# The running maximum's last two steps of an attention kernel, with the ninth chunk's scores in PSUM as an operand of both

## The chip, the core and the metric

The kernel runs on one core of a Trainium2 chip. A core has TensorE (PE in the profile; PEld is its loading of weights), VectorE (DVE), ScalarE (ACT), GpSimd (POOL) and SyncE (SP, which here issues all DMAs), a memory SBUF that all engines use and a small memory PSUM into which PE writes its results. The metric is the time of one execution on the device in microseconds, the median of the runs; lower is better.

## What is computed

The reference is an attention with pooled queries, followed by a soft mixture of experts. Eight batches of eight heads, 1152 keys, 64 elements; the queries are averaged in pairs, so 576 of them are left.

```python
q_pool = q.reshape(B, H, S // factor, factor, D).mean(axis=3)
scores = scale * np.matmul(q_pool, k.transpose(0, 1, 3, 2))
scores = scores - np.max(scores, axis=-1, keepdims=True)
attn = np.exp(scores)
attn = attn / (np.sum(attn, axis=-1, keepdims=True) + 1e-09)
return np.matmul(attn, v).astype(np.float32)
```

The result, 4608 rows of 512, is the x of the mixture: `logits = x @ phi`, a softmax over the rows that gathers x into 32 slots, two matrix products with a ReLU between for each of eight experts, and a softmax over the slots that spreads the result over the rows. All data are 32-bit floats. The maximum of the scores over the keys is the part that the change touches.

## The kernel before

**Units.** Two heads are worked on together, which makes 32 pairs; the 576 queries of a pair are cut into three thirds of 192. A pair's third is a unit: there are 96, and each has scores of 1152 keys by 2 heads by 192 queries. The keys lie on the 128 partitions, in nine chunks of 128, so that one chunk is a block of 128 x 2 x 192 = 128 x 384 numbers.

**A unit's steps**, by the short names of the graph and the methods of class `Unit`:

- `S` (`scores`): PE makes the scores of a tile of chunks in PSUM. The tiles are chunks (0, 1), (2, 3), (4, 5), (6, 7) and (8). There are two PSUM buffers for them, `sc0` and `sc1`, of two banks each, taken in turn. So a tile waits until all that work on the tile two before it are done.
- `C` (`copy`): ACT copies the tile to SBUF, into `s`.
- `X` (`maxi`, L523 to L531): DVE keeps a running maximum `M`, a tile in SBUF with two parts of 384, one for the even and one for the odd chunks. The second tile is compared with the copy of the first, the third and fourth from PSUM with `M`. The ninth chunk stands alone and is compared with the first part, `M[:, 0]`.
- `Xf` (`fold`, L533): DVE folds the two parts of `M` into `M[:, 0]`. In the order of before it stands between the fourth tile and the ninth chunk.
- `mt`, `mc`, `mb` (`max_cols`, `max_red`, `max_rows`): PE transposes the 384 maxima of each partition in three matmuls (m<-ident,M in the profile), DVE reduces them, and PE spreads the result over the partitions.
- `sub`, `exp`: DVE subtracts the maximum from three chunks at a time, ACT takes the exponential.
- `add`, `sums`: GpSimd adds seven of the chunks up (cs in the profile), and PE sums over the partitions with a matrix of ones.
- `av`, `ue`: PE multiplies with the values into `U`, ACT copies the result out.
- `tc`, `eps`, `rcp`, `tr`, `nx`: the sums are turned (DVE, 32 x 32 blocks), inverted (DVE), turned back, and GpSimd multiplies them into the result `xT`.

Three score buffers `s` in SBUF let three units be under way at once.

**The mixture's first half** (class `Moe`) runs between the units, one piece for each batch of twelve units. The expert matrices are loaded into SBUF in pieces of 512 KB, 23 of the 64 during the units and the others where the units' memory comes free. What follows behind the last unit is the mixture's second half.

**The order.** No engine's order is written by hand. `graph` lists every step with its engine, a cost in a model, the steps that it depends on, and a priority: the table `K["t"]` gives a due time for each kind of step, counted from the unit's own time (9.0 us a unit). `plan` goes through the graph as a list scheduler: on each engine, of the steps that can start within `K["wait"]` of the earliest, it takes the one with the least due time; `K["stay"]` is a bonus for a PE step that keeps PE in the mode (row groups, column groups, all of it) it is in. The result is one order of all steps, and the program is written in it; each engine works through its own part strictly in that order. The waits between engines follow from what each step reads and writes.

The profile gives nearly all instructions the line of a helper (L344, the call in `InOrder`), so groups are told apart by the names of their tiles: `M<-M` is `Xf`, `M<-sc,M` with 128x384 is the ninth chunk's `X`, `M<-sc,M` and `M<-sc,s` with 128x768 are the others.

Of the kernel before, what the change touches and what calls it, by code (L numbers as in the profile page):

```python
# [12 lines left out]
ALU = mybir.AluOpType  # L13
# [9 lines left out]
K = dict(  # L23
    unit=9.0,
    bufs=3,
    stay=97.457,
    wait=dict(PE=0.13, ACT=0.445, DVE=0.179, Pool=4.882),
    adds=(7, 7, 2),
    more=3,
    tiles=((0, 1), (2, 3), (4, 5), (6, 7), (8,)),  # L30
    groups=((0, 1, 2), (3, 4, 5), (6, 7, 8)),
    t=dict(
        S=(1044.713, -27.378, 661.778, 130.467, 574.088),
        C=(225.408, -176.587, 488.066, 26.318, 184.372),
        X=(-718.744, -301.904, -170.628, 686.571, 208.197),
        Xf=(730.727,),
        mt=(148.202,),
        mc=(-195.597,),
        mb=(131.38,),
        sub=(-1080.957, -16.471, 937.631),  # L40
        exp=(-1246.656, 343.957, 478.305),
        add=(-198.042, -184.679, 499.318, 714.631, 189.507, 204.651, 492.919, -541.643, -599.421),
        av=(778.115, -59.256, -118.326, -753.912, 731.892, 755.181, 926.264, 54.633, -257.777),
        sums=(248.993, -468.15, 546.677, -343.84, -281.108, -244.636, -433.554, -1124.137, 780.762, 473.892),
        ue=(756.065,),
        tc=(-949.47,),
        eps=(-191.284,),
        rcp=(26.863,),
        tr=(550.849,),
        ad2=(-53.911, -555.751, -604.838, -526.867, -758.418, 550.551, -1200.835, -328.898, -440.675),  # L50
        nx=(106.946,),
        ldk=(-619.286,),
        ldq=(598.38,),
        ldv=(-572.603,),
        qs=(673.048,),
        lg=(-347.354, 583.603, 769.132, 771.621),
        to=(568.435, 368.579, 194.047, -715.38),
        cb=(-19.617, 862.666),
        rm=(693.434, 659.42),
        nm=(-571.082,),  # L60
        ex=(723.911,),
        ns=(-235.664,),
        ce=(449.167,),
        cz=(641.165,),
        cm=(218.808,),
        on=(-345.56, 611.94, -1045.413, -114.604, -959.343, -369.874, 674.366, 739.505, 216.76, -1205.971, -784.9,
            231.495),
        we=(175.597, 148.186),
        ga=(550.866, 285.942, 446.335),
        end_lg=(297.494, 404.708, 205.171, -617.161),  # L70
        end_to=(-1060.395, 611.733, 617.206, 387.095),
        end_cb=(452.212, 686.767),
        end_rm=(-41.937, 690.132),
        end_nm=(-764.111,),
        end_ex=(794.722,),
        end_ns=(1693.028,),
        end_ce=(-656.049,),
        end_cz=(283.723,),
        end_cm=(-111.35,),
        end_on=(-245.398, -314.311, 700.307, -568.747, 642.619, -769.575, 431.084, 234.287),  # L80
        end_we=(196.041, -1145.853),
        end_ga=(619.182, -375.889, -765.507),
        fin_lg=(193.516, 208.183),
        fin_to=(-933.237, -176.561),
        fin_cb=(677.952, 123.947),
        fin_rm=(47.158,),
        fin_nm=(-321.662,),
        fin_ex=(537.275,),
        fin_ns=(474.34,),
        fin_ce=(684.257,),  # L90
        fin_cz=(538.018,),
        fin_cm=(778.587,),
        fin_on=(655.715, -822.063, -169.447, 107.564),
        fin_we=(557.048, -643.386),
        fin_ga=(827.62, -315.564, 319.142),
        fin_gs=(-237.215,),
    ),
)
LAT = 0.05
# [12 lines left out]
def dve_t(n):  # L112
    return 0.075 + 0.001042 * n, 0.16 + 0.001042 * n
# [12 lines left out]
def graph(K, B, HP, NT3, Q, NW):  # L126
# [3 lines left out]
    TI, GR = K["tiles"], K["groups"]  # L130
# [15 lines left out]
    def op(name, eng, cost, deps=(), bank=None, take=False, give=False, key=None):  # L146
        if not isinstance(cost, tuple):
            cost = (cost, cost + (0.17 if eng == "PE" else 0.1))
        mode = MODES.get(name[0], "full") if eng == "PE" else None
        ops[name] = (eng, cost, place(*name) if key is None else key, [d for d in deps if d], bank, take, give, mode)  # L150
# [5 lines left out]
    def old(ok, *name):  # L156
        return name if ok else None
# [21 lines left out]
    for u in range(NU):  # L179
        n, na = u // NT3, adds[u]  # L180
        for i, tl in enumerate(TI):
            g = len(TI) * u + i - 2
            d = [old(g >= 0, "C", g // len(TI), g % len(TI)), old(g >= 0 and g % len(TI), "X", g // len(TI), g % len(TI))]
            d += [("S", u, i - 1)] if i else [("qs", n), ("x", "ldk", n), old(u, "S", u - 1, len(TI) - 1)]
            d += [("x", "k2")] if u == 0 and tl[0] == KF else [("qs2",)] if (u, i) == (1, 0) else []
            op(("S", u, i), "PE", 0.00168 * Q * len(tl), d)
            d = [("S", u, i)]
            for c in tl:
                d += [("av", u - NB, c), freed(u - NB, c)] if u >= NB else []
            op(("C", u, i), "ACT", act_t(2 * Q * len(tl)), d)  # L190
            if i:
                before = ("X", u, i - 1) if 1 < i < len(TI) - 1 else ("C", u, 0) if i == 1 else ("Xf", u)
                op(("X", u, i), "DVE", dve_t(2 * Q * len(tl)), [("C", u, i), before] + [old(u and i == 1, "mt", u - 1)])
            if i == len(TI) - 2:
                op(("Xf", u), "DVE", dve_t(2 * Q), [("X", u, i)])
        b = ("m", u)
        op(("mt", u), "PE", 0.33, [("X", u, len(TI) - 1)], b, take=True)
        op(("mc", u), "DVE", (0.465, 0.55), [("mt", u), old(u > 1, "mb", u - 2)], b)
        op(("mb", u), "PE", 0.34, [("mc", u)], b)
        for g, cs in enumerate(GR):  # L200
            op(("sub", u, g), "DVE", dve_t(2 * Q * len(cs)), [("mb", u)], b, give=g == len(GR) - 1)
            op(("exp", u, g), "ACT", (1.065, 1.175), [("sub", u, g)])
        for c in range(NC):
            e = [("exp", u, group_of[c])]
            if 0 < c <= na:
                d = e + ([("add", u, c - 1)] if c > 1 else [("exp", u, 0), old(u > 1, "sums", u - 2, NC)])
                op(("add", u, c), "Pool", pool_t(2 * Q), d)
            op(("av", u, c), "PE", 0.00168 * Q, e + [("av", u, c - 1) if c else old(u, "ue", u - 1), old(c == 0, "x", "ldv", n)])
        op(("ue", u), "ACT", act_t(Q), [("av", u, NC - 1), old(u, "nx", u - 1)])
        c0, end = na + 1, ("add", u, na) if na else ("exp", u, 0)  # L210
        items = []
        if u == NU - 1 and K["more"]:
            items, c0, end = [(na, end)], na + 2 + K["more"], ("ad2", u, na + 1 + K["more"])
            for c in range(na + 2, c0):
                op(("ad2", u, c), "DVE", dve_t(2 * Q), [("exp", u, group_of[c]), ("ad2", u, c - 1) if c > na + 2 else ("exp", u, group_of[na + 1])])
        items = [(c, ("exp", u, group_of[c])) for c in range(c0, NC)] + items + [(NC, end)]
        for i, (c, d) in enumerate(items):
            op(("sums", u, c), "PE", 0.00168 * Q, [d, old(i, "sums", u, items[i - 1][0])], ("n", u), take=i == 0)
        op(("tc", u), "DVE", (0.295, 0.375), [("sums", u, NC), old(u, "eps", u - 1)], ("n", u), give=True)
        op(("eps", u), "ACT", (0.2, 0.31), [("tc", u), old(u > 1, "tr", u - 2)])  # L220
        op(("rcp", u), "DVE", (0.09, 0.18), [("eps", u)])
        op(("tr", u), "DVE", (0.29, 0.375), [("rcp", u), old(u > 1, "nx", u - 2)])
        b = u // (NT3 * HP) - 2
        d = [("tr", u), ("ue", u)] + [old(b >= 0, "on", b, j, 0) for j in range(6)] + [old(b >= 0, "lg", b, j, 0) for j in range(2)]
        op(("nx", u), *(("Pool", pool_t(Q)) if u < NU - 1 else ("DVE", dve_t(Q))), d)
    for i, (b, tiles, halves) in enumerate(parts(B)):
# [7 lines left out]
        before = old(0 < i < B, "we", i - 1, 0)  # L234
# [115 lines left out]
def pooled_attention_soft_moe(ctx: ExitStack, tc: tile.TileContext, q, k, v, phi, w1, w2, out):  # L350
# [149 lines left out]
    class Unit:  # L500
# [22 lines left out]
        def maxi(self, i):  # L523
            if i == 1:
                self.M = un.tile([P, 2, 2, QU], F32, name=f"M{self.u}", tag="M", bufs=1)
            n = len(TI[i])
            ps = self.ps[i][:, :, :n * QU].rearrange("p h (c q) -> p c h q", c=n)
            if n == 2:
                dve.tensor_tensor(self.M, ps, self.s[:, 0:2] if i == 1 else self.M, op=ALU.max)
            else:  # L530
                dve.tensor_tensor(self.M[:, 0], ps[:, 0], self.M[:, 0], op=ALU.max)  # L531

        def fold(self):  # L533
            dve.tensor_tensor(self.M[:, 0], self.M[:, 0], self.M[:, 1], op=ALU.max)

        def max_cols(self, bank):
            M = self.M[:, 0].rearrange("p h q -> p (h q)")
# [426 lines left out]
```

## Time and profile before

| | before |
|---|---|
| median of three runs | 986.83 us (986.08 to 987.94) |
| the profiled execution | 987.6 us |
| its span, first to last instruction | 985.8 us |
| mean granted clock of PE | 0.992 |
| busy: PE, DVE, POOL, ACT | 951.1, 902.6, 794.9, 762.3 us |
| HBM traffic over the span | 101 GB/s |

The profile is of one execution. An engine's busy time is the sum of its instructions' spans, overlaps counted once; a group's line gives operation, output<-inputs, the shape, the number of instructions, then the busy time in us and the mean of one in ns, and behind the bar the idle time of the engine before these instructions with what ended most of it. A timeline's line gives the start in us, the time taken in us, the engine, what was done, and how many instructions were merged; a bracket holds the engine's idle time before it and who ended that. PE's ends are modelled, so a busy PE may still hold pauses.

### The profile page before, as it was taken

To read this page: it belongs to the slowest core of one execution; us is meant where nothing else is said; L and a number is where in the kernel's file an instruction comes from. 1 tells how busy PE (TensorE), PEld (TensorE's weight loads), DVE (VectorE), ACT (ScalarE), POOL (GpSimd) and SP (SyncE) were. 2 spreads that over 40 slices of the span, in tenths; PEclk is the share of its full clock that TensorE was granted. 3 is DMA by queue.
4 is the path that set the end of the run, shared out by engine and by line. 5 is a ranking of instruction groups with operands and counts; after the bars stand their busy time and mean duration, and the time that the engine had idled before them with its cause. 6 is when DMAs were issued, how large, how long until landed. Compare 5 with 4: busy or idle time off the path is not lost.

```text
span 985.8 us, 23762 instructions
## 1 busy us (share of the span) xinstructions
PE 951.1 (96%) x9358; PEld 676.1 (69%) x9358; DVE 902.6 (92%) x1307; ACT 762.3 (77%) x1120; POOL 794.9 (81%) x815
## 2 busy tenths in 40 slices
PE   6999999999999999999999999999999999999995
PEld 4666777767776777677777677777776677776542
DVE  5999999999999999999999999999999999999423
ACT  4878888888878888788878788778878788877323
POOL 2899888898889898898889988899888988888200
PEclk8999999999999999999999999999999999999998
DMA  5132232232223222223122212121221221123898
GB/s 171 49 116 82 83 116 82 84 115 74 92 71 116 94 99 88 95 70 117 52 70 73 73 49 68 55 74 52 70 74 54 68 74 49 49 90 128 320 409 339
DMA packets 27681, 101.22 MB, mean 103 GB/s; under 512 B 3505, under 2 KB 4017, under 8 KB 27569
## 3 DMA queue, kind: packets, MB, share of 16 engines
q1 hardware_dynamic: 27568, 99.69, 29.4%
q8 instruction: 74, 1.21, 0.5%
q14 instruction: 39, 0.31, 0.1%
HBM read 90.24 MB, written 9.44 MB: 101 GB/s over the span
## 4 chain that ended last, share of the span: by engine, by line
PE 84%; DVE 12%; issue 1%; ACT 0%; DMA 0%; SPq 0%; DVEq 0%; ACTq 0%
PE sc L344 32%; PE U L344 27%; PE m L344 20%; DVE M L344 7%; PE b L344 5%; DVE s L344 2%; DVE zt L344 1%; DVE mc L344 1%; DVE slot L344 0%; DVE rc L344 0%; ACT s L344 0%; DMA k<-in_k_dram 0%; PE idle L344 0%; DVE c L344 0%; DVE rr L344 0%
## 5 line engine op out<-in xcount | busy, mean ns | idle before, releaser
L344 POOL TENSOR_TENSOR cs<-cs,s 128x384 f32<-128x384 f32 x571 | 586.8, 1028 | 61.7 <-ACT s L344 26.3
L344 ACT COPY s<-sc 128x768 f32<-128x768 f32 (+1 forms) x480 | 344.6, 733 | 91.8 <-PE sc L344 86.1
L344 PE MATMUL sc<-qs,k 64*128 64x192 f32 x3456 | 389.0, 349 | 20.9 <-DVE M L344 16.3
L344 DVE TENSOR_TENSOR s<-s,m 128x1152 f32<-128x1152 f32 x288 | 382.3, 1338 | 3.3 <-PE m L344 2.3
L344 ACT ACTIVATE s<-s 128x1152 f32<-128x1152 f32 x288 | 336.2, 1168 | 45.3 <-DVE s L344 45.1
L344 PEld LDWEIGHTS sc<-qs,k 64*128 64x128 f32 x3456 | 275.6, 188 | 117.0 <-issue 73.8
L344 PE MATMUL U<-s,v 128*64 128x192 f32 x3456 | 344.6, 333 | 0.9 <-ACT Us L344 0.9
L344 PEld LDWEIGHTS U<-s,v 128*64 128x64 f32 x3456 | 227.7, 136 | 73.3 <-issue 47.6
L344 DVE TENSOR_TENSOR M<-sc,M 128x768 f32<-128x768 f32 (+1 forms) x288 | 235.3, 817 | 6.3 <-ACT s L344 2.5
L344 POOL TENSOR_TENSOR cs<-s 128x384 f32<-128x384 f32 x96 | 96.8, 1008 | 33.9 <-ACT s L344 33.8
L344 DVE TENSOR_TENSOR M<-sc,s 128x768 f32<-128x768 f32 x96 | 91.0, 947 | 4.3 <-ACT s L344 4.3
L344 DVE TENSOR_TENSOR M<-M 128x384 f32<-128x384 f32 x96 | 71.2, 742 | 0.3
L344 POOL TENSOR_TENSOR xT<-rr,Us 128x192 f32<-128x192 f32 x95 | 57.1, 601 | 12.7 <-DVE rr L344 10.2
L344 POOL TENSOR_TENSOR qs<-q 128x576 f32<-128x576 f32 x31 | 54.6, 1761 | 13.3 <-DMA q<-in_q_dram 13.3
L344 DVE TENSOR_REDUCE mc<-m 128x3 f32<-128x384 f32 x96 | 53.4, 556 | 11.4 <-PE m L344 7.4
L344 PE MATMUL m<-ident,M 128*128 128x128 f32 x288 | 52.8, 293 | 0.0
L344 PE MATMUL m<-ident,mc 128*128 128x128 f32 x288 | 51.9, 289 | 0.0
L344 PE MATMUL m<-s,ones 128*64 128x192 f32 x388 | 48.7, 330 | 0.2 <-ACT s L344 0.2
L344 PE MATMUL m<-cs,ones 128*64 128x192 f32 x384 | 47.5, 326 | 0.0
L344 ACT COPY Us<-U 128x192 f32<-128x192 f32 x96 | 30.7, 320 | 21.7 <-PE U L344 20.9
L344 PEld LDWEIGHTS m<-ident,mc 128*128 128x128 f32 x288 | 29.2, 136 | 26.6 <-DVE mc L344 24.1
L344 PEld LDWEIGHTS m<-ident,M 128*128 128x128 f32 x288 | 30.1, 141 | 21.6 <-issue 21.6
(92 smaller groups left out, 499.6 us busy)
## 6 DMA issues: line engine op xcount, KB each, us to landing
w<-in_moe_w_dram SPq DMA_DIRECT2D x64, 512.0 KB, 5.4
v<-in_v_dram SPq DMA_DIRECT2D x32, 576.0 KB, 3.8
k<-in_k_dram SPq DMA_DIRECT2D x31, 576.0 KB, 3.8
q<-in_q_dram SPq DMA_DIRECT2D x31, 576.0 KB, 3.8
out_dram<-ob SPq DMA_DIRECT2D x24, 384.0 KB, 6.0
q<-in_q_dram SPq DMA_DIRECT2D x1, 384.0 KB, 6.4
k<-in_k_dram SPq DMA_DIRECT2D x1, 320.0 KB, 4.9
k<-in_k_dram SPq DMA_DIRECT2D x1, 256.0 KB, 2.9
```

The lines of the kernel that those rows point to most:

```text
L344: return self.tc.keep_in_program_order(op(*args, **kwargs))
```

## The change

In the method for the running maximum, the ninth chunk no longer goes into `M[:, 0]`: its maximum with `M[:, 0]` is written over the scores in PSUM, and the fold then takes the maximum of that and `M[:, 1]` into `M[:, 0]`. So the ninth chunk comes ahead of the fold. In the graph, the fold now depends on the ninth chunk, the transposes on the fold, and the PSUM buffer of the ninth chunk is given back by the fold. The table of due times, the bonus `stay` and the times `wait` have new values throughout, so that the order of all steps is another. Number, shape and data of all other operations are the same.

```diff
-    stay=97.457,
-    wait=dict(PE=0.13, ACT=0.445, DVE=0.179, Pool=4.882),
+    stay=344.932,
+    wait=dict(PE=0.084, ACT=0.259, DVE=0.255, Pool=0.318),
...
-        S=(1044.713, -27.378, 661.778, 130.467, 574.088),
-        C=(225.408, -176.587, 488.066, 26.318, 184.372),
-        X=(-718.744, -301.904, -170.628, 686.571, 208.197),
-        Xf=(730.727,),
+        S=(2388.548, -94.193, 2355.419, 2292.606, -219.496),
+        C=(2649.137, 2739.454, 3306.242, 2568.215, 2210.822),
+        X=(-718.744, 41.55, 2544.783, 3038.773, 3019.567),
+        Xf=(2420.829,),
...
             d = [old(g >= 0, "C", g // len(TI), g % len(TI)), old(g >= 0 and g % len(TI), "X", g // len(TI), g % len(TI))]
+            d += [old(g >= 0 and g % len(TI) == len(TI) - 1, "Xf", g // len(TI))]
...
-                before = ("X", u, i - 1) if 1 < i < len(TI) - 1 else ("C", u, 0) if i == 1 else ("Xf", u)
+                before = ("X", u, i - 1) if i > 1 else ("C", u, 0)
                 op(("X", u, i), "DVE", dve_t(2 * Q * len(tl)), [("C", u, i), before] + [old(u and i == 1, "mt", u - 1)])
-            if i == len(TI) - 2:
-                op(("Xf", u), "DVE", dve_t(2 * Q), [("X", u, i)])
+        op(("Xf", u), "DVE", dve_t(2 * Q), [("X", u, len(TI) - 1)])
         b = ("m", u)
-        op(("mt", u), "PE", 0.33, [("X", u, len(TI) - 1)], b, take=True)
+        op(("mt", u), "PE", 0.33, [("Xf", u)], b, take=True)
...
             else:
-                dve.tensor_tensor(self.M[:, 0], ps[:, 0], self.M[:, 0], op=ALU.max)
+
+                self.top = ps[:, 0]
+                dve.tensor_tensor(self.top, self.top, self.M[:, 0], op=ALU.max)
 
         def fold(self):
-            dve.tensor_tensor(self.M[:, 0], self.M[:, 0], self.M[:, 1], op=ALU.max)
+            dve.tensor_tensor(self.M[:, 0], self.top, self.M[:, 1], op=ALU.max)
```

More of the change, by code (lines that the diff above doesn't have):

```diff
@@ L32 @@
     t=dict(
-        S=(1044.713, -27.378, 661.778, 130.467, 574.088),
-        C=(225.408, -176.587, 488.066, 26.318, 184.372),
-        X=(-718.744, -301.904, -170.628, 686.571, 208.197),
-        Xf=(730.727,),
[L37 to L96, printed above, removed]
+        S=(2388.548, -94.193, 2355.419, 2292.606, -219.496),
+        C=(2649.137, 2739.454, 3306.242, 2568.215, 2210.822),
@@ new lines @@
+        X=(-718.744, 41.55, 2544.783, 3038.773, 3019.567),
+        Xf=(2420.829,),
+        mt=(108.212,),
+        mc=(2834.326,),
+        mb=(357.261,),
+        sub=(2554.368, 2777.459, 3141.454),
+        exp=(2989.515, 2742.131, 2760.717),
+        add=(-198.042, 2806.366, 2691.244, 2455.169, 2982.071, 2750.805, 2789.269, 2832.224, -599.421),
+        av=(2746.723, 2428.358, 2392.407, 122.273, 2706.594, 2907.997, 2728.152, 193.704, -87.967),
+        sums=(248.993, -468.15, 101.759, -343.84, -281.108, -244.636, -433.554, 32.153, 2812.114, 369.166),
@@ new lines @@
+        ue=(2111.732,),
+        tc=(2995.475,),
+        eps=(-193.75,),
+        rcp=(-83.517,),
+        tr=(2755.622,),
+        ad2=(-53.911, -555.751, -604.838, -526.867, 2247.684, 2996.492, 85.086, -328.898, -440.675),
+        nx=(2766.587,),
+        ldk=(324.978,),
+        ldq=(3216.414,),
+        ldv=(-24.147,),
+        qs=(2956.952,),
+        lg=(2368.498, 2686.237, 3086.901, 182.464),
+        to=(3083.591, 2792.944, 2930.818, 2510.319),
+        cb=(2719.978, 2928.296),
+        rm=(2748.01, 258.088),
@@ new lines @@
+        nm=(2832.009,),
+        ex=(-128.418,),
+        ns=(2772.413,),
+        ce=(3121.69,),
+        cz=(2769.817,),
+        cm=(3200.587,),
+        on=(3097.6, 2506.278, 3054.228, 446.422, 2486.677, 2547.485, 2860.756, -93.424, 3100.505, 2694.192,
+            3179.786, 243.542),
+        we=(2631.977, 2680.618),
+        ga=(2926.036, 2801.7, 2712.536),
+        end_lg=(3020.693, -97.35, 2441.615, 2619.398),
+        end_to=(2726.63, -63.379, 2652.638, 2157.507),
+        end_cb=(101.937, 2494.248),
@@ new lines @@
+        end_rm=(2678.247, 2864.44),
+        end_nm=(2374.775,),
+        end_ex=(2655.735,),
+        end_ns=(2969.979,),
+        end_ce=(2929.199,),
+        end_cz=(3117.05,),
+        end_cm=(2896.398,),
+        end_on=(2567.266, 2821.336, 2621.07, 2651.936, 2871.573, 3152.89, 2747.133, 2424.348),
+        end_we=(2627.177, 2721.688),
+        end_ga=(2869.597, -375.889, 2849.104),
+        fin_lg=(2808.896, 3072.292),
+        fin_to=(2543.921, 2224.667),
+        fin_cb=(3639.957, 2729.612),
@@ L97 @@
+        fin_rm=(3023.064,),
+        fin_nm=(3006.424,),
+        fin_ex=(2881.713,),
+        fin_ns=(2929.914,),
+        fin_ce=(3322.203,),
+        fin_cz=(3098.918,),
+        fin_cm=(2739.156,),
+        fin_on=(3812.858, 3235.474, 3085.749, 2848.33),
+        fin_we=(3149.484, 2802.356),
+        fin_ga=(2993.364, -315.564, 2524.846),
+        fin_gs=(3664.586,),
     ),
```

## The prediction, made before the change was run

> **What bounds the kernel now.** I read the page first, then the windows of the middle, then the groups by form, and last the timeline unit by unit. The page's head and one window of 100 us in the middle:
>
> ```profile
> span 985.8 us, 23762 instructions
> PE 951.1 (96%) x9358; PEld 676.1 (69%) x9358; DVE 902.6 (92%) x1307; ACT 762.3 (77%) x1120; POOL 794.9 (81%) x815
> ...
> 500.00:600.00 100.00, 98.52 (x978) 71.77 (x974) 97.69 (x137) 81.94 (x117) 89.07 (x91) 1.00 0.22 67
> ```
>
> The window's columns are the stretch, its length, then busy time of PE, weight loads, DVE, ACT and POOL, the granted clock (1.00, so no throttle), DMA share and GB/s. Two engines are full at once, PE with 98.52 and DVE with 97.69 of 100 us. ACT has 18 us to spare, and DMA is idle for four fifths. Neither full engine is the answer by itself: the question is which of them sets the pace of one unit, and that cannot be read from shares. So I went to the operations that the diff touches, by form:
>
> ```profile
> L344 DVE TENSOR_TENSOR s<-s,m 128x1152 f32<-128x1152 f32 x288 | 382.3, 1338 | 3.3 <-PE m L344 2.3
> ...
> L344 DVE TENSOR_TENSOR M<-sc,M 128x768 f32<-128x768 f32 x192 | 182.3, 949 | 4.3 <-ACT s L344 2.5
> ...
> L344 DVE TENSOR_TENSOR M<-M 128x384 f32<-128x384 f32 x96 | 71.2, 742 | 0.3
> ...
> L344 DVE TENSOR_TENSOR M<-sc,M 128x384 f32<-128x384 f32 x96 | 53.1, 553 | 2.0 <-PE U L344 0.3
> ```
>
> M<-M is the fold of the maximum's two parts, both in SBUF. M<-sc,M with 384 elements is the ninth chunk, one operand in PSUM. They have the same number of elements and the same operation, yet the fold costs 742 ns against 553. The view of tile M says what kind of difference that is:
>
> ```profile
> L344 DVE TENSOR_TENSOR M<-sc,M x288: 517/951/960, 9.4 to 903.5; 128x768 f32<-128x768 f32 x96, 128x384 f32<-128x384 f32 x48
> ...
> L344 DVE TENSOR_TENSOR M<-M x96: 515/552/1360, 12.1 to 902.9; 128x384 f32<-128x384 f32 x96
> ```
>
> The three numbers are least, median and most. The fold's least and median, 515 and 552 ns, are those of the PSUM form; but some folds take up to 1360, while nothing in the first row, twice as many elements included, is over 960. So the fold is not slow: it is sometimes held up, and the operations with one operand in PSUM are not. By what, the timeline shows, GpSimd beside two folds:
>
> ```profile
> 518.42 1.01 POOL L344 TENSOR_TENSOR cs<-cs,s 128x384 f32<-128x384 f32 x1
> 519.39 1.78 POOL L344 TENSOR_TENSOR qs<-q 128x576 f32<-128x576 f32 x1
> ...
> 528.06 2.26 POOL L344 TENSOR_TENSOR cs<-cs,s 128x384 f32<-128x384 f32 x2
> ```
> ```profile
> 519.38 0.52 DVE L344 TENSOR_TENSOR M<-M 128x384 f32<-128x384 f32 x1
> 519.83 0.19 DVE L344 RECIPROCAL rc<-rc 128x6 f32<-128x6 f32 x1
> 519.93 0.55 DVE L344 TENSOR_TENSOR M<-sc,M 128x384 f32<-128x384 f32 x1
> ...
> 528.14 1.33 DVE L344 TENSOR_TENSOR M<-M 128x384 f32<-128x384 f32 x1
> ...
> 537.71 0.52 DVE L344 TENSOR_TENSOR M<-M 128x384 f32<-128x384 f32 x1
> ```
>
> The fold at 519.38 begins as a GpSimd addition ends (518.42 + 1.01 = 519.43) and takes 0.52. The one at 528.14 begins 0.08 after an addition began, and takes 1.33: the addition's time and its own. The two additions behind it take 2.26 instead of twice 1.01, so the wait goes both ways.
>
> Whether this time is on the path is settled by the pace. These are the transposes of the finished maximum, one group for each unit, and the busy time of one unit with a short fold and the next with a long one:
>
> ```profile
> 512.72 0.55 PE L344 MATMUL m<-ident,M 128*128 128x128 f32 x3
> 521.49 0.55 PE L344 MATMUL m<-ident,M 128*128 128x128 f32 x3
> 531.06 0.55 PE L344 MATMUL m<-ident,M 128*128 128x128 f32 x3
> 539.82 0.55 PE L344 MATMUL m<-ident,M 128*128 128x128 f32 x3
> ```
> ```profile
> 512.72:521.49 8.77, 8.77 (x89) 6.34 (x87) 8.63 (x13) 7.17 (x10) 7.10 (x8) 1.00 0.00 0
> 521.49:531.06 9.57, 8.97 (x88) 6.33 (x87) 9.49 (x13) 7.45 (x11) 8.93 (x11) 1.00 0.34 91
> ```
>
> The intervals are 8.77, 9.57 and 8.76 us; the folds in them took 0.52, 1.33 and 0.52. The unit is longer by 0.80 where its fold is longer by 0.81. A held-up fold is paid in full. In the long unit PE is busy for 8.97 of 9.57, with a wait of 0.60; in the short one for 8.77 of 8.77. So DVE sets the pace where the fold is held up, and PE is the floor, at about 8.77, where it is not.
>
> **The change part by part.** The profiled execution took 987.6 us, with a span of 985.8; it lies 0.8 above the median of the three timed runs, 986.83.
>
> *The fold.* It goes from two SBUF operands to one in PSUM and one in SBUF. The nearest row is the 384 form of M<-sc,M, which has these operands: 553 ns. Saved are 742 - 553 = 189 ns for each of 96 units, 18.1 us. The pairs of intervals above say that it counts in full. The bounds: the least fold on record, 515, would give 227 x 96 = 21.8; but then the unit would stand at the floor of PE, where a short fold stands already, so this is the most that the fold can give by itself.
>
> [...]
>
> *The ninth chunk.* It now writes its result into PSUM, over its own operand, and moves ahead of the fold. No row has DVE writing PSUM. From below, the fold's 515 ns (a gain of 38 ns, 3.6 us in all); from above, the case that reading and writing one PSUM tile can't go side by side, so that 384 elements cost like 768: 949 ns, a loss of 396 x 96 = 38.0 us. I take 553, that is nothing, as the nearest row differs in the output alone; the upper bound is a rival.
>
> It must also not run before ACT has copied the ninth chunk out of the same tile. That order stands in the graph before the change too. What moves is the time: the ninth chunk starts where the fold did. In the unit at 519.38 that is 0.95 us after ACT had finished the copies of the last two tiles, and in the unit at 528.14 it is 0.90 after:
>
> ```profile
> 517.16 1.27 ACT L344 COPY s<-sc 128x768 f32<-128x768 f32 x2
> ...
> 526.06 1.18 ACT L344 COPY s<-sc 128x768 f32<-128x768 f32 x2
> ```
>
> (The rows merge an even tile and the ninth chunk: 517.16 + 1.27 = 518.43 and 526.06 + 1.18 = 527.24.) So nothing is queued behind a new wait there. Where ACT comes later, DVE stands with the transposes and subtractions that are queued behind the ninth chunk.
>
> *The buffer.* The tile of scores with the ninth chunk is given back after two operations instead of one. Who waits for it is the second tile of the next unit on PE, and behind it all of PE's queue:
>
> ```profile
> 528.69 0.92 PE L344 MATMUL sc<-qs,k 64*128 64x192 f32 x8
> 530.21 0.92 PE L344 MATMUL sc<-qs,k 64*128 64x192 f32 x8 [0.60 <-DVE M L344]
> ```
>
> In the order of before the pair fold, ninth chunk becomes ninth chunk, fold: the last of the two ends at the same place or, with 189 ns saved, earlier. I cost it at nothing. The cover is that pair's being close together, with one reciprocal of 0.10 from start to start between them (519.83 to 519.93). If the new order puts a subtraction between them, the tile is held 1.3 us longer.
>
> *GpSimd.* Its additions no longer meet the fold: in the group of 571 additions the mean is 1028 ns, where the first additions of the units take 1008. That frees some 571 x 0.02 = 11 us on an engine with 11 of 100 us idle; it is not on the path and counts nothing.
>
> ```profile
> L344 POOL TENSOR_TENSOR cs<-cs,s 128x384 f32<-128x384 f32 x571 | 586.8, 1028 | 61.7 <-ACT s L344 26.3 <-issue 2.2
> L344 POOL TENSOR_TENSOR cs<-s 128x384 f32<-128x384 f32 x96 | 96.8, 1008 | 33.9 <-ACT s L344 33.8
> ```
>
> *The order.* All priorities are new, and I cannot read the order from them. The prices that it can move are those of PE's visits to a kind of work. A lone tile of eight score matmuls takes 528.69 to its end 529.61, of which the last matmul's own time overlaps with the next job; two in one go take less than twice that:
>
> ```profile
> 519.93 1.63 PE L344 MATMUL sc<-qs,k 64*128 64x192 f32 x16
> ...
> 521.96 0.92 PE L344 MATMUL sc<-qs,k 64*128 64x192 f32 x8
> 522.81 0.54 PE L344 MATMUL m<-ident,mc 128*128 128x128 f32 x3
> ```
>
> From start to start the lone tile takes 522.81 - 521.96 = 0.85, the pair 521.49 - 519.93 = 1.56: one visit more costs 2 x 0.85 - 1.56 = 0.14 on this side, and about as much where the other work is cut in two, some 0.28 in all (an estimate). I take no visit more and none less, as both sides are open.
>
> *Sum:* 987.6 - 18.1 = 969.5 for a profiled execution, and 0.8 less for the median: 968.7 us. The work behind the last unit is filled by the loading of weights, which starts when the units end, so it moves along and changes nothing: the page's slices of 24.6 us show the traffic rise only there.
>
> ```profile
> GB/s 171 49 116 82 83 116 82 84 115 74 92 71 116 94 99 88 95 70 117 52 70 73 73 49 68 55 74 52 70 74 54 68 74 49 49 90 128 320 409 339
> ```
>
> **The rivals.**
>
> *A better order.* With the fold out of the way, PE is the floor, and DVE has 8.77 - 8.63 = 0.14 us idle in a short unit beside it. One visit less in half of the units saves 48 x 0.28 = 13.4 more: 955.3. For it: the priorities are made for the graph as it is now. Against: with 0.14 of slack on DVE for each unit, 13.4 us is all that DVE allows.
>
> *Part of it is lost on PE.* The new order keeps PE as full as now but lets ACT's copy or the buffer's return come late in a third of the units, by the 0.2 to 0.3 us which the bracketed waits show, or adds a visit in a third: 32 x 0.28 = 9.0, 977.7.
>
> *No change:* the saving and the new order's price cancel, 986.8. That the fold does not get rid of GpSimd is the other way to it: it still has one operand in SBUF, but 288 operations with such operands show no case over 960 ns.
>
> *Slower, by the order.* PE bridges the later return of the buffer by one further visit in every unit: 96 x 0.28 = 26.9, less 18.1: 995.6. It decides from 65 units on (18.1 / 0.28). For it: the second score tile follows 0.1 us behind the ninth chunk's end, so the return is timed to the point; against: the pair ends no later than now.
>
> *Slower, by the write.* The ninth chunk's 949 ns instead of 553: 968.7 + 38.0 = 1006.7. It decides from 189 ns more than the 553 on.
>
> **How the numbers follow.** Forecast 0.58; better order 0.14; part lost 0.11; no change 0.05; slower by the order 0.08, by the write 0.04. What a measurement of this kernel can tell from no change is about 0.2%, 2 us. Faster: 0.58 + 0.14 + 0.11 = 0.83; within: 0.05; slower: 0.12. The forecast's own range is 963 to 974: 20 visits more or fewer make 5.6 us either way, and the fold's bound of 3.7 lies within. The range that is to hold 8 in 10 takes in the better order and the lost part, each with some of its own spread: 952 to 985. Left out are no change, both slower cases and the far end of the better order, some 0.2.
>
> **What would show it.** Right: the fold's row at 515 to 560 ns with no long cases, the ninth chunk's at about 553 with PSUM as its output, units without the mixture's work all at about 8.8 us, DVE's sum down by 18 us, GpSimd's additions at about 1008. Wrong: a ninth chunk far above 553 (the write); PE waits for the maximum or many more short visits in its timeline (the order); intervals over 9 us with a short fold, which would mean that something else than the fold set the pace.

## The result and the profile after

| | before | changed |
|---|---|---|
| median | 986.46 us (985.89 to 987.94, 4 runs) | 970.43 us (968.6 to 971.73, 4 runs) |
| profiled execution, its span | 987.6, 985.8 us | 971.73, 970.0 us |

The ratio is 0.983 with a 95% interval of 0.981 to 0.985: 16 us less, where 18.1 were forecast. The page's head, a window in the middle (PE, weight loads, DVE, ACT and POOL, as before), and the groups by form that the change touches:

```profile
span 970.0 us, 23842 instructions
PE 941.9 (97%) x9358; PEld 677.3 (70%) x9358; DVE 884.8 (91%) x1307; ACT 754.4 (78%) x1120; POOL 769.9 (79%) x815
```
```profile
500.00:600.00 100.00, 99.84 (x1002) 73.38 (x998) 97.03 (x140) 83.35 (x122) 87.71 (x93) 1.00 0.18 57
```
```profile
L344 POOL TENSOR_TENSOR cs<-cs,s 128x384 f32<-128x384 f32 x571 | 573.1, 1004 | 54.9 <-ACT s L344 15.2 <-issue 7.2 <-POOL cs L344 0.3
...
L344 DVE TENSOR_TENSOR M<-sc,M 128x384 f32<-128x384 f32 x96 | 52.1, 543 | 0.1
...
L344 DVE TENSOR_TENSOR sc<-sc,M 128x384 f32<-128x384 f32 x96 | 51.6, 537 | 1.3 <-DVE zt L344 0.2
```

The names have changed places: `M<-sc,M` with 384 elements is now the fold, `sc<-sc,M` the ninth chunk. The fold takes 543 ns instead of 742, which is 19.1 us in 96 units; the ninth chunk, into PSUM, 537 instead of 553. DVE's busy time is 17.8 us less, but that is not these two groups alone, as the last rows of this section show. GpSimd's additions are at 1004 ns instead of 1028. The view of tile M gives least, median and most:

```profile
L344 DVE TENSOR_TENSOR M<-sc,M x288: 515/951/958, 10.0 to 888.5; 128x768 f32<-128x768 f32 x96, 128x384 f32<-128x384 f32 x48
...
L344 DVE TENSOR_TENSOR sc<-sc,M x96: 529/534/567, 12.4 to 887.9; 128x384 f32<-128x384 f32 x96
```

The pace of the units without the mixture's work, from one group of transposes to the next, and the busy time of one of them and of one with the mixture's work:

```profile
520.37 0.55 PE L344 MATMUL m<-ident,M 128*128 128x128 f32 x3
529.07 0.55 PE L344 MATMUL m<-ident,M 128*128 128x128 f32 x3
537.78 0.55 PE L344 MATMUL m<-ident,M 128*128 128x128 f32 x3
546.49 0.55 PE L344 MATMUL m<-ident,M 128*128 128x128 f32 x3
```
```profile
520.37:529.07 8.70, 8.70 (x88) 6.33 (x86) 8.39 (x13) 7.14 (x11) 7.58 (x9) 1.00 0.40 129
489.93:501.00 11.07, 9.94 (x99) 7.19 (x97) 10.69 (x18) 8.88 (x17) 8.08 (x8) 1.00 0.47 153
```

The units of 9.57 us are gone; these all take 8.70 to 8.71, with PE busy throughout and DVE idle for 0.3. The other row is what the forecast had not seen: a unit of 11 us in which PE waits for more than one. The timeline shows why:

```profile
495.53 1.41 POOL L344 TENSOR_TENSOR qs<-q 128x576 f32<-128x576 f32 x1 [1.35 <-PE sc L344]
495.61 1.35 DVE L344 SCALAR_TENSOR_TENSOR rmax<-bm,rmax 128x1 f32<-128x1 f32 x1
...
496.90 1.00 POOL L344 TENSOR_TENSOR cs<-s 128x384 f32<-128x384 f32 x1
...
496.99 0.92 DVE L344 TENSOR_TENSOR nm<-zero,rmax 128x1 f32<-128x1 f32 x1
...
499.49 0.92 PE L344 MATMUL sc<-qs,k 64*128 64x192 f32 x8 [0.97 <-DVE M L344]
```

The mixture's running maximum (`rmax`) and its negative (`nm`) work on one number for each partition, and take 1.35 and 0.92 us: both begin 0.08 to 0.09 after an operation of GpSimd began, and both end as that one ends. Like the fold of before, each reads two columns from SBUF at once (`rmax` a third one as its scalar), and the new order sets them beside a busy GpSimd. Six batches show it. Before, the same groups were these:

```profile
L344 DVE SCALAR_TENSOR_TENSOR rmax<-bm,rmax 128x1 f32<-128x1 f32 x7 | 1.5, 220 | 0.2
L344 DVE TENSOR_TENSOR nm<-zero,rmax 128x1 f32<-128x1 f32 x9 | 1.4, 160 | 0.3
```

and after the change:

```profile
L344 DVE SCALAR_TENSOR_TENSOR rmax<-bm,rmax 128x1 f32<-128x1 f32 x7 | 8.3, 1188 | 0.0
L344 DVE TENSOR_TENSOR nm<-zero,rmax 128x1 f32<-128x1 f32 x9 | 6.0, 669 | 0.3
```

That is 8.3 + 6.0 - 1.5 - 1.4 = 11.4 us of DVE, given back in another place.

### The profile page after: what moved, and what is told of

Same layout as the page of the kernel before. It is cut to its first block, busy times and chain, and to the rows that moved or that the text cites. A ratio compares the mean times of both kernels' runs of the same rounds, so it can differ in the third digit from the quotient of the medians.

```text
span 970.0 us, 23842 instructions
## 1 busy us (share of the span) xinstructions
PE 941.9 (97%) x9358; PEld 677.3 (70%) x9358; DVE 884.8 (91%) x1307; ACT 754.4 (78%) x1120; POOL 769.9 (79%) x815
## 3 DMA queue, kind: packets, MB, share of 16 engines
HBM read 90.24 MB, written 9.44 MB: 103 GB/s over the span
## 4 chain that ended last, share of the span: by engine, by line
PE 89%; DVE 7%; DMA 1%; issue 1%; ACT 0%; SPq 0%; DVEq 0%
PE sc L344 34%; PE U L344 29%; PE m L344 20%; PE b L344 5%; DVE M L344 3%; DVE s L344 2%; DVE rmax L344 1%; DMA w<-in_moe_w_dram 1%; DVE nm L344 1%; DVE mc L344 0%; DVE sc L344 0%; DMA k<-in_k_dram 0%; PE idle L344 0%; DVE bm L344 0%; ACT s L344 0%
## 5 line engine op out<-in xcount | busy, mean ns | idle before, releaser
L344 POOL TENSOR_TENSOR cs<-cs,s 128x384 f32<-128x384 f32 x571 | 573.1, 1004 | 54.9 <-ACT s L344 15.2
L344 PE MATMUL sc<-qs,k 64*128 64x192 f32 x3456 | 383.8, 347 | 14.2 <-DVE M L344 9.7
L344 PE MATMUL U<-s,v 128*64 128x192 f32 x3456 | 336.6, 332 | 0.2 <-ACT s L344 0.2
L344 PEld LDWEIGHTS U<-s,v 128*64 128x64 f32 x3456 | 232.4, 137 | 65.1 <-issue 36.8
L344 DVE TENSOR_REDUCE mc<-m 128x3 f32<-128x384 f32 x96 | 53.2, 554 | 20.6 <-PE m L344 18.8
L344 POOL TENSOR_TENSOR qs<-q 128x576 f32<-128x576 f32 x31 | 43.9, 1415 | 21.6 <-DMA q<-in_q_dram 13.6
L344 DVE TENSOR_TENSOR sc<-sc,M 128x384 f32<-128x384 f32 x96 | 51.6, 537 | 1.3 <-DVE zt L344 0.2
```

What stands on the lines that cost most here:

```text
L344: return self.tc.keep_in_program_order(op(*args, **kwargs))
```

## The experiments

Theory A is the forecast's: a fold with both operands in SBUF is held up by GpSimd, and the excess is paid in full. Theory B: the new order brings the gain. Each experiment was timed in turns with the kernel before on its chip; the ratio is to that.

**The old order with the new operations.** The order of before is kept, with the two changed operations, and in it the two steps change places: the ninth chunk goes to the fold's place where its copy stands ahead of that in the list, which holds for 95 of the 96 units.

```diff
-        if name[0] != "x":
+        if name[0] == "C" and name[2] == 4:
+            copied.add(name[1])
+        if name[0] == "Xf":
+            if name[1] in copied:
+                U_(name[1]).maxi(4)
+                early.add(name[1])
+        elif name[0] == "X" and name[2] == 4:
+            if name[1] not in early:
+                U_(name[1]).maxi(4)
+            U_(name[1]).fold()
+        elif name[0] != "x":
             do[name[0]](*name[1:], bank)
```

> The order of before, with the changed operations: the ninth chunk's maximum goes into PSUM at the place where the fold stood, and the fold takes the ninth chunk's old place. Theory A (the fold with both operands in SBUF is held up by GpSimd's additions, and its excess is paid in full): the fold at 515 to 560 ns with no long case, intervals of 8.76 us in all units without the mixture's work, 96 x (742 - 543) ns = 19 us less than before: 966 to 969 us, and so as fast as the changed kernel or up to 4 us faster. Theory B (the gain comes from the new order, the operations matter little): 980 to 987 us.

Measured: 976.44 us, ratio 0.989 (0.988 to 0.990). Neither theory's number. The units without the mixture's work do what A says:

```profile
506.32 0.55 PE L344 MATMUL m<-ident,M 128*128 128x128 f32 x3
515.10 0.55 PE L344 MATMUL m<-ident,M 128*128 128x128 f32 x3
523.88 0.55 PE L344 MATMUL m<-ident,M 128*128 128x128 f32 x3
```

8.78 us each, none of 9.57. What is missing lies in the other units. This is from DVE's waits in this kernel (us in total, times, longest):

```profile
DVE sc L344 <- ACT s L344: 7.8, 22, 0.5
```

The ninth chunk, moved ahead, now stands before ScalarE's copy of the same tile is done, in the first three units of each batch from the second on, by 0.30 to 0.46 us; before the change its group had 2.0 us of idle time in all, none of it put down to this copy, as the fold filled that time. Two intervals in which such a wait falls took 9.57 and 9.62 us, where they took 9.44 and 9.47 before:

```profile
456.71 0.55 PE L344 MATMUL m<-ident,M 128*128 128x128 f32 x3
466.28 0.55 PE L344 MATMUL m<-ident,M 128*128 128x128 f32 x3
475.90 0.55 PE L344 MATMUL m<-ident,M 128*128 128x128 f32 x3
```

The last experiment but one tests whether that is the loss.

**The changed kernel again**, for the same chip.

> The changed kernel once more, for the comparison with the others on the same chip. Both theories: 968 to 973 us.

Measured: 970.0 us, ratio 0.983 (0.981 to 0.984).

**The new order, with SBUF as the operand.** Twice: with the change's sequence, and with the old one.

```diff
-                self.top = ps[:, 0]
-                dve.tensor_tensor(self.top, self.top, self.M[:, 0], op=ALU.max)
+                dve.tensor_tensor(self.M[:, 0], ps[:, 0], self.M[:, 0], op=ALU.max)
...
-            dve.tensor_tensor(self.M[:, 0], self.top, self.M[:, 1], op=ALU.max)
+            dve.tensor_tensor(self.M[:, 0], self.M[:, 0], self.M[:, 1], op=ALU.max)
```

> The new order, ninth chunk ahead of the fold as in the change, but the ninth chunk's maximum goes into SBUF again, so that the fold has both operands in SBUF. Theory A: in the changed kernel's trace an operation of GpSimd has another 450 ns to run, on average, when the fold begins, 43 us in all; the fold's mean goes to 800 to 1100 ns with cases over 1300, and the time to 990 to 1013 us, slower than the kernel before. Theory B (the order brings the gain): 968 to 975 us.

Measured: 991.96 us, ratio 1.005 (1.004 to 1.007).

The second run has the same two operations, and in the order of the steps:

```diff
-        if name[0] != "x":
+        if name[0] == "X" and name[2] == 4:
+            U_(name[1]).fold()
+        elif name[0] == "Xf":
+            U_(name[1]).maxi(4)
+        elif name[0] != "x":
             do[name[0]](*name[1:], bank)
```

> The new order, with the fold in SBUF at the ninth chunk's place and the ninth chunk, into SBUF, at the fold's place, which is the sequence and the operands of before. Theory A: GpSimd has another 453 ns to run at that place on average; the fold's mean at 800 to 1100 ns and the time at 990 to 1013 us. Theory B: 968 to 975 us.

Measured: 993.31 us, ratio 1.007 (1.004 to 1.010). The fold's least, median and most, and its group, in the first and the second of these two:

```profile
L344 DVE TENSOR_TENSOR M<-M x96: 553/804/1310, 12.7 to 910.0; 128x384 f32<-128x384 f32 x96
L344 DVE TENSOR_TENSOR M<-M 128x384 f32<-128x384 f32 x96 | 85.6, 891 | 0.1
```
```profile
L344 DVE TENSOR_TENSOR M<-M x96: 512/1022/1355, 12.9 to 910.2; 128x384 f32<-128x384 f32 x96
L344 DVE TENSOR_TENSOR M<-M 128x384 f32<-128x384 f32 x96 | 86.3, 899 | 0.1
```

Theory B falls: without the new operands the new order makes the kernel slower, by 4.4 and 5.8 us against the 987.53 of the kernel before on this chip. More of its folds meet GpSimd (means of 891 and 899 ns instead of 742, 14 to 15 us in all), and `rmax` and `nm` are held up as in the changed kernel; what the rest of the order gains or hides was not taken apart. The changed operations are worth 987.5 - 976.4 = 11.1 us in the old order, with the change of places, and the operand alone 992.0 - 970.0 = 22.0 us in the new one.

**GpSimd busy, but not reading**, in the kernel before.

```diff
-            pool.tensor_tensor(self.cs, self.s[:, 0] if c == 1 else self.cs, sv, op=ALU.add)
+            for _ in range(2):
+                pool.memset(self.cs, 1.0)
```

> The kernel before, with each of GpSimd's additions of chunks replaced by two fills of the same tile, which write SBUF and read nothing. The sum over those chunks is left out. If the fold is held up by what GpSimd reads: no fold over 560 ns, no unit of 9.57 us among those without the mixture's work, 967 to 971 us. If GpSimd's being busy, or its writing, holds the fold up, or if something else does: folds up to 1300 ns remain, and the time is 983 to 989 us.

Measured: 969.55 us, ratio 0.983 (0.981 to 0.984). The fills and the fold:

```profile
L344 POOL MEMSET cs<- 128x384 f32 x1334 | 553.4, 419 | 84.2 <-PE m L344 18.6
```
```profile
L344 DVE TENSOR_TENSOR M<-M x96: 514/517/678, 12.1 to 884.7; 128x384 f32<-128x384 f32 x96
```

The order, the operands and the sequence are those of before; GpSimd is busy with fills for 553 us, and the fold has a median of 517 and goes up to 678 at most, over the 560 expected, where it went to 1360. The folds over 560 are 15, and every one of them begins while GpSimd makes the sums of the queries, which still read SBUF:

```profile
89.61 1.42 POOL L344 TENSOR_TENSOR qs<-q 128x576 f32<-128x576 f32 x1
...
90.78 0.67 DVE L344 TENSOR_TENSOR M<-M 128x384 f32<-128x384 f32 x1
```

Of the others, 33 begin during a fill, and none of these takes over 559 ns. The fills differ from the additions in more than the reading: two of them take 0.84 us where an addition takes 1.0, and they do not wait for ScalarE's exponentials. That does not show in the pace: intervals without a long fold before the change stay what they were (8.76, 9.47 and 9.84 us before; 8.76, 9.46 and 9.84 here). So in this kernel it is GpSimd's reading of SBUF that holds up an operation that reads SBUF twice (a fold takes up to 1360 ns beside the additions, and 559 at most where it begins during a fill), and 17 us is about what that cost the kernel before, small operations of the mixture included (the adding of a constant to its sums, `cz`, goes from 588 to 163 ns here, its running sum, `rsum`, from 326 to 187).

**The changed kernel with a running maximum that reads SBUF once.**

```diff
-    rmax = [keep.tile([P, 1], F32, name=f"rmax{i}") for i in range(2)]
+    bmax = [keep.tile([P, 3], F32, name=f"bmax{i}") for i in range(2)]
+    rmax = [bmax[1][:, 2:3], bmax[0][:, 2:3]]
...
-                dve.scalar_tensor_tensor(new, bm[0], prev, bm[1], op0=ALU.max, op1=ALU.max)
-            dve.tensor_tensor(self.nm, zero, new, op=ALU.subtract)
+            dve.tensor_reduce(new, bmax[self.i % 2][:, :3 if self.i else 2], axis=AX.X, op=ALU.max)
...
         def expo(self):
+            act.activation(self.nm, rmax[self.i % 2], AF.Identity, bias=zero, scale=-1.0)
```

> The changed kernel, with the mixture's running maximum made so that no operation of it reads two operands from SBUF on VectorE: the two halves' maxima and the old maximum stand in one tile of three columns and are reduced in one operation, and ScalarE makes the negative. In the changed kernel six of these maxima took 1.35 us and six negatives 0.92, where they took 0.22 and 0.16 before the change. If those are the same kind of hold-up and are on the path: the maximum at 0.15 to 0.25 us in all batches, the units of 11.03 us at 9.2 to 10.0, and 958.5 to 964 us. If they are hidden behind PE: 968 to 973 us.

Measured: 962.78 us, ratio 0.976 (0.974 to 0.977). The reduction's times, and the pace of the unit that took 11.03, in the changed kernel first and then here:

```profile
L344 DVE TENSOR_REDUCE bmax<-bmax x9: 148/150/156, 153.9 to 898.4; 128x1 f32<-128x3 f32 x8, 128x1 f32<-128x2 f32 x1
```
```profile
489.93 0.55 PE L344 MATMUL m<-ident,M 128*128 128x128 f32 x3
500.96 0.55 PE L344 MATMUL m<-ident,M 128*128 128x128 f32 x3 [0.16 <-DVE M L344]
```
```profile
488.14 0.55 PE L344 MATMUL m<-ident,M 128*128 128x128 f32 x3
497.90 0.55 PE L344 MATMUL m<-ident,M 128*128 128x128 f32 x3
```

9.76 us instead of 11.03, six times 1.27, is 7.6 us, and 970.4 - 962.8 is 7.6 (7.2 with the 970.0 of the second measurement). The hold-up of the two small operations was on the path, and this is the fastest kernel of the study.

**The same maximum in the old order**, a control: the old order with the new operations, and this edit.

> The old order with the changed operations, with the same new running maximum of the mixture. In this order the maximum and the negative took 0.22 and 0.16 us, so nothing is held up there; it shows what the rewriting does by itself. 974 to 977 us, that is as without it; 965 us or less would mean that the rewriting gains for another reason than the hold-up.

Measured: 978.59 us, ratio 0.992 (0.991 to 0.993), 2 us slower than without it and 1.6 above the range expected; one unit of most batches takes 10.10 us instead of 9.84 there, and why is open. The rewriting itself gains nothing; the gain above is the hold-up's.

**The changed kernel without the fold.**

```diff
-                self.top = ps[:, 0]
-                dve.tensor_tensor(self.top, self.top, self.M[:, 0], op=ALU.max)
+                dve.tensor_tensor(self.M[:, 0], ps[:, 0], self.M[:, 0], op=ALU.max)
...
-            dve.tensor_tensor(self.M[:, 0], self.top, self.M[:, 1], op=ALU.max)
+            pass
```

> The changed kernel without the fold: the ninth chunk's maximum goes into SBUF as the end of the running maximum, and the odd chunks' part is left out of it. VectorE has 0.54 us less in each unit. If PE is now the floor of the units without the mixture's work: these stay at 8.6 to 8.71 us, and the time goes down by 0 to 12 us, 958 to 970. If VectorE still sets the pace: the units go to 8.25, 45 us less, 925 us.

Measured: 967.44 us, ratio 0.980 (0.979 to 0.982). A window of it, and the pace:

```profile
500.00:600.00 100.00, 100.00 (x999) 73.61 (x998) 92.76 (x125) 83.72 (x120) 88.76 (x94) 1.00 0.19 60
```
```profile
517.24 0.55 PE L344 MATMUL m<-ident,M 128*128 128x128 f32 x3
525.94 0.55 PE L344 MATMUL m<-ident,M 128*128 128x128 f32 x3
534.65 0.55 PE L344 MATMUL m<-ident,M 128*128 128x128 f32 x3
```

DVE is busy for 92.76 of 100 us instead of 97.03, and the units stay at 8.70 to 8.71: PE is the floor there now. With the fold left out altogether, 3 us are gained.

**The old order, with the old steps where the copy comes late.**

```diff
-                self.top = ps[:, 0]
-                dve.tensor_tensor(self.top, self.top, self.M[:, 0], op=ALU.max)
+                self.top = ps[:, 0] if self.u % 12 not in (0, 1, 2, 4) else self.M[:, 0]
+                dve.tensor_tensor(self.top, ps[:, 0], self.M[:, 0], op=ALU.max)
```

(In the units 0, 1, 2 and 4 the fold then stands ahead of the ninth chunk, as before.)

> The old order with the changed operations, but in four units of each twelve (the first, second, third and fifth, where the ninth chunk's maximum waited for ScalarE's copy, 22 waits of 7.8 us in all) the steps of before: fold in SBUF, then the ninth chunk. If the wait for the copy is what the old order loses by the ninth chunk's moving ahead: the waits disappear, the units of 9.57 and 9.62 go back to 9.41 to 9.47, and the time is 972 to 975 us, 2 to 4 less than with the changed operations everywhere. If something else loses it: 976 to 980 us, as folds in SBUF may be held up again.

Measured: 972.94 us, ratio 0.986 (0.984 to 0.987), against 0.989 with the new steps everywhere. The two intervals that took 9.57 and 9.62 are back at 9.43 and 9.47:

```profile
455.40 0.55 PE L344 MATMUL m<-ident,M 128*128 128x128 f32 x3
464.83 0.55 PE L344 MATMUL m<-ident,M 128*128 128x128 f32 x3
474.30 0.55 PE L344 MATMUL m<-ident,M 128*128 128x128 f32 x3
```

The wait for the copy is real and worth about 3 us, a part of which is the fifth unit's: there the ninth chunk had waited 0.10 us for VectorE's own last step and not for the copy, and its interval goes from 10.51 to 10.41. Half of the 32 folds that stay in SBUF here are held up again, to 1017 ns at most; from the second batch on these are the folds of a batch's first two units, and their intervals, 9.08 and 9.43, are much as with the fills (9.08 and 9.41). Another 3 us are lacking to the 969.55 us of the kernel with the fills. Most of them are not in the steps changed here: from the second batch to the seventh a batch takes 111.0 us, and 110.9 with the fills, and of the 3.4 us between the two spans 2.7 lie ahead of the second batch. There even two profiles of the changed kernel differ by 1.3 us, in the start of the first transposes (14.5 and 15.8).

**The running sum on ScalarE as well**, on top of the running maximum that reads SBUF once.

```diff
-                dve.scalar_tensor_tensor(rsum, rsum, self.corr, self.bs, op0=ALU.mult, op1=ALU.add)
+                act.activation(rsum, rsum, AF.Identity, scale=self.corr, bias=self.bs)
```

> The changed kernel with the free maximum of the mixture, and the mixture's running sum made on ScalarE too; on VectorE it took 0.45 us in six batches, where two operands in SBUF had taken 0.21 before that. If that hold-up is on the path, 1 to 3 us less than with the free maximum alone: 960 to 962 us. If PE is the floor there, no difference: 962 to 964 us.

Measured: 963.84 us, ratio 0.977 (0.976 to 0.979): no gain over 962.78. The unit's pace is 9.76 as without it. This is that unit in the kernel without the edit, with `rsum` held up in it (0.45 us, where the changed kernel has 0.21):

```profile
488.14:497.90 9.76, 9.76 (x98) 7.15 (x96) 9.13 (x18) 9.12 (x18) 7.91 (x8) 1.00 0.44 148
```

PE is busy for all of it. Here a hold-up is hidden behind PE.

## Why the prediction was right

*What sets the pace.* Right in the units from which it was read. That a held-up fold is paid in full came from three intervals, 8.77, 9.57 and 8.76; with the fills the intervals of 9.6 are 8.76, and the kernel is 17 us faster for 19 us less of folds (742 to 544 ns). But it does not hold everywhere. One of the five long folds in each batch from the second on is hardly paid: that of the batch's second unit, about 1000 ns, takes 517 with the fills, and its interval only goes from 9.44 to 9.41 us. In the new order 33 us of folds (891 to 543 ns) were worth 22 us.

*The fold's term*, 18.1 us by 553 ns. The row says 543, which is 19.1. Right, and so is the floor: 8.70 us with PE full; without the fold it is no lower.

*The operand in PSUM.* The fold's change from SBUF to PSUM in one operand got no price of its own, only the nearest row's 553 ns. The rows bear that out, if operations at the same place of the order are compared. Between the same two neighbours (`zt` and `rc`) the fold with both operands in SBUF has a median of 516 ns in the run with the fills, and the ninth chunk with one in PSUM 519 in the new order with SBUF as the operand. Behind another step of the running maximum both take 558. In these rows the operand in PSUM costs 3 ns at most.

*The ninth chunk into PSUM.* Taken at 553, measured 537; the rival that reading and writing one tile doubles it is out.

*ScalarE's copy.* Costed at nothing from two units without the mixture's work. That held in the changed kernel, with 1.3 us of idle time before the ninth chunk, but only because the new order makes room: in the old order there are 7.8 us of waits, about 3 of them on the path. The lost-part rival had the mechanism, with its place in the units that I had not looked at.

*GpSimd.* Here the argument had a gap. The forecast looked at the operations that the diff touches, and at no others. `rmax` and `nm` read two columns from SBUF too, at 220 and 160 ns and in the list of small groups; a new order can set them beside GpSimd, and did. That cost 7.6 us. It freed two others in turn, `cz` and `rsum`, which had been held up before (4.1 and 2.6 us before, 1.6 and 1.7 after).

*The sign of 18 us less of DVE.* Measured 17.8, and a hit by luck: the fold and the ninth chunk give 20.6, `rmax` and `nm` take 11.4 back, and the rest, 8.6, comes from other groups (3.3) and from instructions that overlap more (5.3).

*The order.* Taken at nothing, with both sides open. It was not nothing: with the new operations it is worth 976.4 - 970.0 = 6.4 us, and with the free maximum in both orders 978.6 - 962.8 = 15.8 us. From the third batch to the sixth the two orders take the same, 111.5 us a batch, as the small operations' loss eats up the gain there; the 6.4 us lie in the first two batches and the last. So the mechanism was right, but that the total came out within 2 us is in part luck: two things that were costed at nothing, the order's gain and the small operations' loss, went against each other.

## What to carry to other kernels

Where one operation on VectorE takes a wide range of times at the same shape, compare its least with its most, look at what GpSimd is doing in the long cases, and count how many of its operands lie in SBUF. To see whether such an excess is on the path, compare the length of neighbouring repeats with the length of the operation in them; busy shares of 97 and 98% do not tell. A new order must be looked at for every operation with two operands in SBUF, however small: one number per partition waited 1.1 us in the changed kernel.

## What the hardware showed that was not expected

- An operation on one number for each partition was held up for 1.13 us (1.35 instead of 0.22), until GpSimd's operation of 1.41 us ended; that it is small did not shorten the wait.
- In two cases what began first went on and the other waited. With the fills, a fold that began 1.17 us after a sum of the queries took 0.67 us and the sum its 1.42. Before the change, the sum at 519.39 began 0.01 after a fold; the fold took 0.52 and the sum 1.78. So GpSimd lost time as well: its sums of the queries (qs, 128x576) took 1761 ns on average before and 1415 after.

```profile
L344 POOL TENSOR_TENSOR qs<-q 128x576 f32<-128x576 f32 x31 | 54.6, 1761 | 13.3 <-DMA q<-in_q_dram 13.3
```
```profile
L344 POOL TENSOR_TENSOR qs<-q 128x576 f32<-128x576 f32 x31 | 43.9, 1415 | 21.6 <-DMA q<-in_q_dram 13.6 <-PE sc L344 8.1
```

- VectorE writes PSUM over the operand that it reads there at little cost: 537 ns on average for 384 elements, against 521 for the same step of the same order where it writes SBUF (the first of the two runs of the new order with SBUF as the operand).
